# Unread products in six array tilings behind the last products of an attention and gated-layer kernel

## The chip, the cores and the metric

The kernel runs on one core of a Trainium2 chip. The metric is device time in microseconds (us). One execution was also recorded by the hardware profiler; its own time and its span (first to last recorded instruction) stand beside the runs below.

The engines are named as in the profile: PE is TensorE's products, PEld its weight loads, DVE VectorE, ACT ScalarE, POOL GpSimd, SP SyncE, which issues the transfers. A "q" behind a name means the engine's queue (semaphores, drains, issues).

## What is computed

One input `x` (2048 rows of 512) goes through two branches, which a gate mixes row by row:

```python
def reference(A_x, A_wq, A_wk, A_wv, A_wo, B_x, B_w_gate, B_w_up, B_w_down, gate_w):
    x = A_x
    g = sigmoid((x * gate_w).sum(-1, keepdims=True))
    # a: 32 query heads of 16, one key and one value head
    q = (x @ wq) in heads;  k = x @ wk;  v = x @ wv
    p = softmax(einsum("bhqd,bkd->bhqk", q, k) * 16 ** -0.5)
    a = (einsum("bhqk,bkd->bhqd", p, v) in rows) @ wo
    # b: gated layer of width 1792
    b = (sigmoid(x @ w_gate) * (x @ w_up)) @ w_down
    return g * a + (1 - g) * b
```

The kernel takes all of `x` from `A_x`, as the reference does.

## The kernel before

The rows of `x` are cut into four blocks of 512. Each block has eight units of attention (four heads of 512 queries each), 32 units in all. For a unit the kernel makes the scores twice: once to find each row's maximum (L1159 on TensorE, L1161 on VectorE), and once, turned, for the exponential (L1168, then L1170 on ScalarE). The products with the values and a column of ones (`v_aug`, L1029) give the outputs and their sums. Beside these run the products of the gated layer and of the output projection (`fill`, L1133).

Most operands are split into a high and a low part of type fp32r. Their products contract over 64 rows and stand in pairs, one in the upper half of the array's rows and one in the lower (`TOP` and `BOT`), each with a bank of its own in PSUM: a tiling of 64x128 (rows by columns of a tile). L1029's products are fp32, contract over 128 rows and have 32 columns: a tiling of 128x32, four tiles side by side. The trace writes such a product in fp32 as two records, one for each pass. The first projections (L874) take the whole array, 128x128.

The order of all this is a string of codes (`ORDER`, L683 to L729), which `plan` (L732) walks through; every engine then executes its part of that order in sequence. What follows the plan is written out by hand in `tile_kernel`, L1190 to L1227, for the last unit alone:

- L1192 names the bank of the last value products `end`, and the seven others `rest`; `ps` (L1193) are the last four of these.
- ScalarE copies `end` (L1196), TensorE turns it into `rest[0]` and `rest[1]` (L1198), VectorE divides by the sums (L1203, L1205), TensorE turns it back into `rest[2]` and `rest[1]` (L1207), and ScalarE copies that to `o_last` (L1209).
- The **last products** (L1214) project `o_last`, 16 products of the tiling 64x32 over 512 columns, into the four banks `ps`.
- VectorE (L1224), and for one tile ScalarE and GpSimd (L1220, L1221), add the four banks to the four output tiles `ba`, and SyncE stores them by five transfers (L1227).

Behind that comes a closing that the framework makes (in the profile under L1274): SyncE waits for the transfers that are under way, each engine drains, and all meet at a barrier before the program ends.

In the change two operands appear that the kernel has held since its first phase: `ks` (128 rows of 2048, fp32r), the keys, in both halves of the rows, and `v_aug` (128 rows, 16 groups of 32 columns, fp32). `turns` and `pairs` are views that reorder 512 columns as two interleaved runs of 256.

Of the kernel before, what the change touches and what calls it, by code (L numbers as in the profile page):

```python
# [18 lines left out]
P = 128  # L19
# [15 lines left out]
TOP, BOT = slice(0, 64), slice(64, 128)  # L35
HALF = (TOP, BOT)
# [705 lines left out]
def tile_kernel(ctx, tc, x_in, wq, wkv, wo, wg, wu, wd, consts_in, out):  # L742
    nc = tc.nc
# [18 lines left out]
    turns = lambda a: a.rearrange("p (w c) -> p c w", w=2)  # L762
    pairs = lambda a: a.rearrange("p (c w) -> p c w", w=2)
# [125 lines left out]
    v_aug = cp.tile([P, NC, 32], F32, name="v_aug")  # L889
# [16 lines left out]
    for o in (0, 64):  # L906
        nc.vector.tensor_copy(stack_of[:, :, o:o + 48].rearrange("p kc (i d) -> p kc i d", d=DH),
                              some[:, :, :DH].unsqueeze(2).to_broadcast([P, KC, 3, DH]))
        n = 8 if o else 9
# [4 lines left out]
    ks = cp.tile([P, S], F32R, name="ks")  # L914
# [277 lines left out]
    end, rest = banks[end], [bank for i, bank in enumerate(banks) if i != end]  # L1192
# [17 lines left out]
    for i in range(2):  # L1210
        for j in range(4):
            for t in (2 * i, 2 * i + 1):
                r, m = HALF[t % 2], slice(32 * j, 32 * j + 32)
                nc.tensor.matmul(pairs(ps[t][m, :]), o[i][r, m], turns(WS["last"][r]), start=True, stop=True)  # L1214
    BL = [BA.pop((NB - 1, t)) for t in range(NT)]
    for t in (1, 0, 2, 3):
        ba, g = BL[t], gsig[:, n0 + t:n0 + t + 1]
        if t == 1:
# [6 lines left out]
    for t in (0, 2, 1, 3):  # L1225
        for r in (slice(0, D // 2), slice(D // 2, D)) if t == 0 else (slice(0, D),):
            nc.sync.dma_start(out[(n0 + t) * P:(n0 + t + 1) * P, r], BL[t][:, r])  # L1227

# [49 lines left out]
```

## Time and profile before

| | us |
|---|---|
| median of 3 runs (lowest to highest) | 1533.65 (1532.41 to 1535.66) |
| the profiled execution's own time | 1534.46 |
| its span | 1532.7 |
| busy: TensorE products / weight loads | 1520.6 / 977.4 |
| busy: VectorE / ScalarE / GpSimd | 1359.3 / 1160.1 / 624.5 |

In a row of the timeline stand: start in us from the span's start, length of the merged group in us, engine, line, operation, output and inputs, the tiling (rows*columns of a tile), the shape, the number of records, and in brackets the engine's idle time ahead of it and what ended it. Ends of products are modelled, so that products which follow each other overlap in the records. In the instructions of a line stand: engine, operation, number, shortest/median/longest duration in ns, and the first and last start. In the stretches stand: the stretch and its length, busy time of the five rows PE, PEld, DVE, ACT, POOL with their counts, TensorE's granted clock, the share of the transfer engines and GB/s.

### The profile page before, as it was taken

The numbers are of one execution on the slowest core, as the hardware profiler recorded it, in microseconds if no ns is written. First come the engines' busy times: TensorE is split into PE (matmuls) and PEld (weight loads), VectorE is DVE, ScalarE is ACT, GpSimd is POOL, SyncE is SP. The second block draws the span as 40 slices with busy tenths as digits, with TensorE's granted clock in tenths as the row PEclk, the third lists the DMA queues.
The fourth block names the chain that finished last, engine by engine and source line by source line (L and its number), as shares of the span: only waits on it lengthen the run. The fifth ranks groups of instructions, "written<-read, shape, count | busy, mean of one in ns | idle before, by whom it ended". The sixth has DMA issues, their size and how long they took to land. (4 is left out here: it accounts for less than half of the span.)

```text
span 1532.7 us, 33127 instructions
## 1 busy us (share of the span) xinstructions
PE 1520.6 (99%) x12910; PEld 977.4 (64%) x12910; DVE 1359.3 (89%) x2320; ACT 1160.1 (76%) x2287; POOL 624.5 (41%) x585
## 2 busy tenths in 40 slices
PE   9999999999999999999999999999999999999997
PEld 7777666656655666666665666676665566666653
DVE  6999988999999998989899988989989998999742
ACT  4257777878788787778788787777878887868796
POOL 4361633561811163255263136077073115427141
PEclk9999999999999999999999999999999999999999
DMA  7531211221211121123031212013021112212011
GB/s 250 175 107 38 71 44 52 71 91 39 88 41 52 46 82 54 34 74 95 30 96 51 69 39 86 22 63 115 31 81 58 55 44 68 69 40 64 13 54 46
DMA packets 63218, 103.42 MB, mean 67 GB/s; under 512 B 24546, under 2 KB 25058, under 8 KB 63060
## 3 DMA queue, kind: packets, MB, share of 16 engines
q1 hardware_dynamic: 63060, 101.29, 20.8%
q8 instruction: 102, 1.67, 0.4%
q14 instruction: 56, 0.46, 0.1%
HBM read 79.51 MB, written 21.75 MB: 66 GB/s over the span
## 5 line engine op out<-in xcount | busy, mean ns | idle before, releaser
L1161 DVE TENSOR_REDUCE mx<-bank 128x1 f32<-128x512 f32 x2048 | 1249.3, 681 | 110.1 <-PE bank L1159 71.7
L1170 ACT ACTIVATE p<-bank 128x512 f32<-128x512 f32 x2048 | 1033.1, 653 | 84.4 <-PE bank L1168 43.9
L1168 PE MATMUL bank<-qs,ks 64*128 64x512 f32 x2048 | 683.1, 389 | 0.0
L1159 PE MATMUL bank<-ks,qs 64*128 64x512 f32 x2048 | 648.4, 394 | 0.8 <-DMA qs<-qd 0.8
L1029 PE MATMUL bank<-p,v_aug 128*32 128x512 f32 x4096 | 490.5, 598 | 0.0
L1168 PEld LDWEIGHTS bank<-qs,ks 64*128 64x128 f32 x2048 | 348.3, 185 | 108.6 <-DVE mx L1161 33.5
L1159 PEld LDWEIGHTS bank<-ks,qs 64*128 64x128 f32 x2048 | 332.2, 185 | 131.0 <-DVE mx L1161 52.1
L1029 PEld LDWEIGHTS bank<-p,v_aug 128*32 128x32 f32 x4096 | 108.3, 109 | 236.6 <-issue 203.0
L1133 PE MATMUL bank<-wd,hl 64*128 64x512 f32 x1344 | 250.5, 378 | 0.0
L1133 PE MATMUL bank<-x,wg 64*128 64x512 f32 x1344 | 247.8, 378 | 0.1
L1043 POOL TENSOR_TENSOR ou<-ou,ou 128x512 f32<-128x512 f32 x74 | 94.6, 1278 | 370.0 <-ACT ou L1036 370.0
L1133 PE MATMUL bank<-x,wu 64*128 64x512 f32 x1344 | 244.4, 378 | 0.1
L1036 ACT COPY ou<-bank 128x512 f32<-128x512 f32 x105 | 61.7, 588 | 226.2 <-PE bank L1029 187.2
L1133 PEld LDWEIGHTS bank<-wd,hl 64*128 64x128 f32 x1344 | 198.4, 186 | 16.7 <-issue 4.2
L1133 PEld LDWEIGHTS bank<-x,wg 64*128 64x128 f32 x1344 | 194.7, 186 | 16.3 <-issue 2.8
L1133 PEld LDWEIGHTS bank<-x,wu 64*128 64x128 f32 x1344 | 192.5, 186 | 15.6 <-POOL wg L851 1.7
L777 POOL TENSOR_TENSOR wd<-rd,wd 128x512 fp32r<-128x512 f32 x56 | 71.6, 1278 | 4.5
L777 POOL TENSOR_TENSOR hl<-h,hl 128x512 fp32r<-128x512 f32 x56 | 71.6, 1278 | 4.5
L1003 POOL CAST ms<-mm 128x16 fp32r<-128x16 f32 x32 | 6.3, 198 | 158.2 <-DVE mm L996 158.2
L851 POOL TENSOR_TENSOR wg<-rg,wg 128x1024 fp32r<-128x1024 f32 x28 | 66.4, 2370 | 5.7 <-ACT wg L841 3.6
L851 POOL TENSOR_TENSOR wu<-ru,wu 128x1024 fp32r<-128x1024 f32 x28 | 66.4, 2370 | 2.2
L776 POOL CAST hl<-h 128x512 fp32r<-128x512 f32 x56 | 34.2, 610 | 74.9 <-DVE h L1148 74.9
(78 smaller groups left out, 683.0 us busy)
## 6 DMA issues: line engine op xcount, KB each, us to landing
rg<-wg SPq DMA_DIRECT2D x28, 512.0 KB
ru<-wu SPq DMA_DIRECT2D x28, 512.0 KB
rd<-wd SPq DMA_DIRECT2D x28, 512.0 KB
qs<-qd SPq DMA_DIRECT2D x192, 64.0 KB
qd<-q SPq DMA_DIRECT2D x32, 256.0 KB
od<-ou SPq DMA_DIRECT2D x31, 256.0 KB
xf<-x_in SPq DMA_DIRECT2D x16, 256.0 KB
vd<-od SPq DMA_DIRECT2D x32, 128.0 KB
```

What stands on the lines that cost most here:

```text
L776: hi(hl[:, 0, :], raw)
L777: lo.tensor_tensor(hl[:, 1, :], raw, f32(hl[:, 0, :]), op=ALU.subtract)
L851: nc.gpsimd.tensor_tensor(WS[item][:, 1, :], raw, f32(WS[item][:, 0, :]), op=ALU.subtract)
L1003: nc.gpsimd.tensor_copy(hl[:, :, 0, :], mm)
L1029: nc.tensor.matmul(ps[32 * j:32 * j + 32, :], v_aug[:, c, :], PT.pop((u, c, j)), start=start, stop=stop)
L1036: nc.scalar.copy(to, ps)
L1043: nc.gpsimd.tensor_tensor(SUMS[u], SUMS[u], PARTS_OF[u].pop(0), op=ALU.add)
L1133: ins = nc.tensor.matmul(pairs(banks[i]), l, turns(r), start=start, stop=stop)
L1159: nc.tensor.matmul(pairs(banks[i]), qs_t[u % 3][r, pr, part(qt)], turns(ks[r, kb * 512:(kb + 1) * 512]), start=True, stop=True)
L1161: nc.vector.tensor_reduce(MX[u][:, pr, h, qt, kb:kb + 1], banks[i], axis=AX.X, op=ALU.max)
L1168: nc.tensor.matmul(pairs(banks[i]), ks[r, part(c)], turns(qs_t[u % 3][r, pr, :]), start=True, stop=True)
L1170: nc.scalar.activation(p, banks[i], AF.Exp, scale=0.25)
```

## The change

Behind the loop of the last products stands a new piece of code, and nothing else differs:

```diff
@@ -1212,6 +1212,24 @@
             for t in (2 * i, 2 * i + 1):
                 r, m = HALF[t % 2], slice(32 * j, 32 * j + 32)
                 nc.tensor.matmul(pairs(ps[t][m, :]), o[i][r, m], turns(WS["last"][r]), start=True, stop=True)
+    va = v_aug.rearrange("p c r -> p (c r)")
+    spots = [rest[0], rest[1]]
+
+    def rows64():
+        for h in (0, 1, 0, 1):
+            r = HALF[h]
+            nc.tensor.matmul(pairs(spots[h]), ks[r, 0:P], turns(ks[r, 512:1024]), start=True, stop=True)
+
+    def others(halves, cols, n):
+        spots_of = [(r, bank) for r, bank in zip((TOP, BOT) if halves else (slice(0, P),), spots)]
+        for m in range(0, P, cols):
+            for r, bank in spots_of:
+                nc.tensor.matmul(bank[m:m + cols, :n], va[r, m:m + cols], va[r, :n], start=True, stop=True)
+
+    rows64()
+    for halves, cols, n in ((True, 32, 256), (False, 32, 256), (True, 64, 256), (False, 64, 256), (True, P, P), (False, P, P)):
+        others(halves, cols, n)
+        rows64()
     BL = [BA.pop((NB - 1, t)) for t in range(NT)]
     for t in (1, 0, 2, 3):
         ba, g = BL[t], gsig[:, n0 + t:n0 + t + 1]
```

`rows64` is four fp32r products of the tiling 64x128 over 512 columns, two pairs. It stands seven times. Between stand six blocks of fp32 products from `v_aug`, one for each of the tilings 64x32 (8 products), 128x32 (4), 64x64 (4), 128x64 (2), all over 256 columns, and 64x128 (2) and 128x128 (1) over 128 columns: 49 products in all. They write the banks `rest[0]` and `rest[1]`, which nobody reads any more. The lines behind the new piece move down by 18 (L1224 becomes L1242, L1227 becomes L1245, L1274 becomes L1292).

On TensorE, at the end of its order, the difference begins so (`bank_72` and `bank_73` are `rest[0]` and `rest[1]`, `bank_78` and `bank_79` the last two of `ps`; the shapes are those of the output, partitions x columns):

```order
 L1214 MATMUL bank_78<-re_0_19490,o_last_19991 32x512
 L1214 MATMUL bank_79<-re_0_19490,o_last_19991 32x512
-L1274 UNCONDITIONAL_BRANCH
+L1221 MATMUL bank_72<-ks 128x512
+L1221 MATMUL bank_73<-ks 128x512
+L1221 MATMUL bank_72<-ks 128x512
+L1221 MATMUL bank_73<-ks 128x512
+L1227 MATMUL bank_72<-v_aug 32x256
+L1227 MATMUL bank_73<-v_aug 32x256
```

Where the program's branch to its closing stood right behind the last products, the first block of four and the first block of `v_aug` products stand now.

The same engine's last rows, from the fp32 block of the tiling 64x128 to the branch:

```order
+L1227 MATMUL bank_72<-v_aug 128x128
+L1227 MATMUL bank_73<-v_aug 128x128
+L1221 MATMUL bank_72<-ks 128x512
+L1221 MATMUL bank_73<-ks 128x512
+L1221 MATMUL bank_72<-ks 128x512
+L1221 MATMUL bank_73<-ks 128x512
+L1227 MATMUL bank_72<-v_aug 128x128
+L1221 MATMUL bank_72<-ks 128x512
+L1221 MATMUL bank_73<-ks 128x512
+L1221 MATMUL bank_72<-ks 128x512
+L1221 MATMUL bank_73<-ks 128x512
+L1292 UNCONDITIONAL_BRANCH
```

All of the added rows stand on TensorE, ahead of its branch. On SyncE the stores stand where they stood, under new line numbers:

```order
 L1073 DMA bc_19673<-rd_19793 64x1x512 x2
-L1227 DMA out<-ba_0_16465 128x256 x2
-L1227 DMA out<-ba_2_16622 128x512
-L1227 DMA out<-ba_1_16460 128x512
-L1227 DMA out<-ba_3_16627 128x512
-L1274 UNCONDITIONAL_BRANCH
+L1245 DMA out<-ba_0_16465 128x256 x2
+L1245 DMA out<-ba_2_16622 128x512
+L1245 DMA out<-ba_1_16460 128x512
+L1245 DMA out<-ba_3_16627 128x512
+L1292 UNCONDITIONAL_BRANCH
```

No transfer is added, removed or moved against another.

## The prediction

> **What bounds the kernel now.** I read the page's first lines, then the last microseconds in the timeline, then the queues' own end (semaphores and drains), because the change stands behind the last products and can only act there.
>
> ```profile
> span 1532.7 us, 33127 instructions
> PE 1520.6 (99%) x12910; PEld 977.4 (64%) x12910; DVE 1359.3 (89%) x2320; ACT 1160.1 (76%) x2287; POOL 624.5 (41%) x585
> ```
>
> TensorE is busy in 1520.6 of 1532.7 us, so for nearly the whole span more work for it would be paid in full. The end is another matter:
>
> ```profile
> 1523.80 2.39 PE L1214 MATMUL bank<-re,o_last 64*32 64x512 f32 x32
> 1524.36 0.15 PEld L1214 LDWEIGHTS bank<-re,o_last 64*32 64x32 f32 x8 [0.38 <-ACT o_last L1209]
> 1524.90 0.15 PEld L1214 LDWEIGHTS bank<-re,o_last 64*32 64x32 f32 x8 [0.39 <-issue]
> 1525.19 0.88 DVE L1224 SCALAR_TENSOR_TENSOR ba<-bank,gsig,ba 128x256 f32<-128x256 f32 x2 [1.72 <-PE bank L1214]
> 1525.30 0.69 ACT L1220 ACTIVATE pa_last<-bank,gsig 128x512 f32<-128x512 f32 x1 [1.07 <-PE bank L1214]
> 1525.71 3.65 SPq L1227 DMA_DIRECT2D out<-ba  x5
> 1526.06 1.26 POOL L1221 TENSOR_TENSOR ba<-ba,pa_last 128x512 f32<-128x512 f32 x1 [15.06 <-ACT pa_last L1220]
> 1526.28 1.41 DVE L1224 SCALAR_TENSOR_TENSOR ba<-bank,gsig,ba 128x512 f32<-128x512 f32 x2 [0.20 <-PE bank L1214]
> ```
>
> The last products (L1214) end at 1523.80 + 2.39 = 1526.19. Behind them come the additions on VectorE (to 1526.28 + 1.41 = 1527.69) and five stores issued by SyncE (to 1525.71 + 3.65 = 1529.36). TensorE has nothing in the last 6.5 us. What ends the span shows in the instructions of the closing line L1274, and in the DMA queue's waits:
>
> ```profile
> L1274 SPq EVENT_SEMAPHORE  x7: 17/28/2202, 1529.4 to 1532.6; - x7
> L1274 POOLq EVENT_SEMAPHORE  x4: 17/17/17, 1532.0 to 1532.6; - x4
> L1274 SPq DRAIN  x3: 7/7/7, 1531.9 to 1532.2; - x3
> L1274 PEldq DRAIN  x2: 13/994/1975, 1524.4 to 1532.3; - x2
> ```
> ```profile
> SPq L1274 <- DMA out<-ba: 2.2, 1, 2.2
> ```
>
> SyncE waits 2.2 us for the stores to land, drains at 1531.9, and GpSimd gathers all engines at 1532.0. From there to 1532.7 is a fixed closing of 0.7 us that every engine joins. TensorE's first drain begins at 1524.4; of its two durations it must be the 1.975 us one (the other begins at 1532.3, 0.4 us before the end), so TensorE reports done at 1524.4 + 1.975 = 1526.3. **It is early by 1531.9 - 1526.3 = 5.6 us.** That is the cover: added TensorE time is free up to 5.6 us, and every microsecond beyond it moves the end by one.
>
> **The change, part by part.** It removes and moves nothing. It adds 28 products of form 64x128 over 512 columns in seven blocks of four, and between them six blocks of `v_aug` products. They write banks whose readers were done before the last products could start, so no new wait stands on TensorE; the additions, stores and waits of the other engines stay as they were. The output banks of the last products are not touched.
>
> *The 64x128 blocks.* The trace has this very pattern: four half-height products between two runs of L1029, and again in the first phase between full-height products.
>
> ```profile
> 1516.01 1.07 PE L1029 MATMUL bank<-p,v_aug 128*32 128x512 f32 x8
> 1517.01 0.70 PE L1168 MATMUL bank<-qs,ks 64*128 64x512 f32 x4
> 1517.64 0.64 PE L1029 MATMUL bank<-p,v_aug 128*32 128x512 f32 x4
> ```
> ```profile
> 27.64 0.70 PE L1159 MATMUL bank<-ks,qs 64*128 64x512 f32 x4
> 28.27 2.86 PE L874 MATMUL bank<-x,wq 128*128 128x512 f32 x12
> 31.05 0.91 PE L1159 MATMUL bank<-ks,qs 64*128 64x512 f32 x5
> ```
>
> Start to start a block of four takes 1517.64 - 1517.01 = 0.63 us, and 28.27 - 27.64 = 0.63. What a change of tiling takes of that is seen against a stretch without one:
>
> ```profile
> 1513.22 0.38 PE L1168 MATMUL bank<-qs,ks 64*128 64x512 f32 x1
> ...
> 1513.43 0.38 PE L1168 MATMUL bank<-qs,ks 64*128 64x512 f32 x1
> 1513.44 0.59 PE L1133 MATMUL bank<-we,o 64*128 64x512 f32 x2
> 1513.65 0.38 PE L1168 MATMUL bank<-qs,ks 64*128 64x512 f32 x1
> 1513.87 0.38 PE L1133 MATMUL bank<-we,o 64*128 64x512 f32 x1
> 1513.87 0.38 PE L1168 MATMUL bank<-qs,ks 64*128 64x512 f32 x1
> 1514.17 1.07 PE L1029 MATMUL bank<-p,v_aug 128*32 128x512 f32 x8
> ```
>
> Pairs (one product in each half of the rows) follow at about 0.215 us (1513.22, .43, .65, .87); the pair ahead of another tiling holds the next start off by 0.30 (1513.87 to 1514.17), so a switch costs about 0.09. Two pairs are 0.43; the remaining 0.2 of a block is the switch behind it and the first weights, loaded in the open (0.11).
>
> *The blocks between.* A run of eight L1029 records is two passes over 512 columns (four column tiles side by side) and takes 1517.01 - 1516.01 = 1.00. Its passes come at:
>
> ```profile
> 1518.10 0.13 PEld L1029 LDWEIGHTS bank<-p,v_aug 128*32 128x32 f32 x4 [0.30 <-issue]
> 1518.53 0.13 PEld L1029 LDWEIGHTS bank<-p,v_aug 128*32 128x32 f32 x4 [0.30 <-issue]
> 1518.95 0.13 PEld L1029 LDWEIGHTS bank<-p,v_aug 128*32 128x32 f32 x4 [0.30 <-ACT p L1170]
> ```
>
> That is 0.43 a pass, and 1.00 - 0.86 = 0.14 for coming and going. Over 256 columns I halve the pass, 0.215:
> - 128x32, four products: 0.43 + 0.14 = **0.57**. The form is in the trace; only its length is not.
> - 64x32, eight products: L1214 has this form, and its passes come at 0.54 (1524.36 to 1524.90). If the rate is lower, a pass over 256 columns takes 0.27 and the block 0.68; if 0.11 is a fixed price of a pass, 0.43 + 0.22 + 0.14 = 0.79. I take **0.72**.
> - 64x64 (four products) and 128x64 (two): neither is in the trace. Below, the 128x32 block's 0.57; above, the dear 64x32 reading, 0.79. 128x64 fills the full height like 128x32 and has only longer weights (some 0.03 more in the open): **0.60**. 64x64 has both halves of the rows: **0.65**.
> - 64x128 over 128 columns in fp32: the tiling of its neighbours, so I count no switch. Two passes at half of 0.215 are 0.22, with a little for weights **0.25**, and the neighbours save one switch and one bare weight load, 0.2. If a change of type were a switch too, it would be 0.42 with nothing saved.
> - 128x128 over 128 columns in fp32: the nearest rows are four transposes of that size,
>
> ```profile
> 39.37 0.66 PE L946 MATMUL bank<-consts,vt 128*128 128x128 f32 x4
> 39.83 2.83 PE L874 MATMUL bank<-x,wkv_s 128*128 128x512 f32 x12
> ```
>
>   0.46 for four, some 0.11 each. Two passes, a switch and bare weights: 0.22 + 0.09 + 0.09 = **0.40**, between 0.33 and 0.50.
>
> *The sum.* In the rows above the next tiling starts 0.07 before the modelled end of the run ahead (1516.01 + 1.07 = 1517.08 against 1517.01), so the first added product starts at 1526.19 - 0.07 = 1526.12. Six blocks of four: 6 x 0.63 = 3.78. The blocks between: 0.72 + 0.57 + 0.65 + 0.60 + 0.25 + 0.40 - 0.2 = 2.99. The last block of four ends 0.70 after its start. TensorE's last product ends at 1526.12 + 3.78 + 2.99 + 0.70 = 1533.59. Its drain follows 0.1 behind (1526.3 against 1526.19), and I allow 0.1 for one more semaphore on SyncE (they take 17 to 28 ns with the steps between): 1533.8 in place of 1531.9. **The end moves by about +1.9 us**, from a span of 1532.7 to 1534.6. With the cheap ends (0.57, 0.57, 0.57, 0.57, 0.22, 0.33, less 0.2) it is 1.5; with the dear ones (0.79, 0.60, 0.79, 0.79, 0.42, 0.50, nothing saved) 2.8.
>
> The profiled execution took 1534.46, 1.8 more than its span; by it the change gives 1536.4. It lies 0.8 above the median of the three runs, 1533.65, so on the scale of the runs I say 1533.65 + 1.9 = **1535.6**, 0.12% more. One may ask whether TensorE still runs at its full clock so late:
>
> ```profile
> 1530.00:1530.50 0.50, 0.00 (x0) 0.00 (x0) 0.00 (x0) 0.00 (x0) 0.00 (x0) 1.00 1.04 393
> 1530.50:1531.00 0.50, 0.00 (x0) 0.00 (x0) 0.00 (x0) 0.00 (x0) 0.00 (x0) 0.66 0.16 57
> ```
>
> The granted clock (third figure from the end) holds 1.00 to 1530.5, over 4 us after the last product, and falls only then. With TensorE kept at work it should not fall.
>
> *A rule against the trace.* The rows above price a switch at 0.09 us. The Trainium skill, "TensorEngine Tiling (Array Packing)", Key Properties, says that a change of tiling mode, not merely of tile, drains the array. The trace agrees that it costs, and shows that the drain mostly hides behind the tail of the products ahead; by a rule of free switches, 12 x 0.09 = 1.1 us would fall out of the sum and leave +0.8.
>
> **The rivals.**
> 1. *All of it is hidden.* If neither switches nor first weights cost anything, the blocks are bare streaming: seven at 0.43, four at 0.43, two at 0.22 are 5.2 us; with 0.16 for the last product to run out (0.38 - 0.215) TensorE ends near 1531.5 and the stores still land last: +0, 1533.65. For it: SyncE's wait for the stores is the longest at the end. Against it: 0.63, not 0.43, for a block of four, in two places. That the products are not there at all would look the same, but they stand in TensorE's order.
> 2. *The unseen tilings are dear; it ends slower.* The switches into and out of 64x64 and 128x64, out of 64x32 and around the fp32 64x128 block are in no row. If at these eight the array ran empty (0.38 - 0.215 = 0.16 of tail) and weights were then loaded bare (0.19, the length of L874's loads below), each would take 0.35 in place of 0.1: 8 x 0.25 = +2.0, in all +3.9, or 1537.6. It decides from 1.2 us above my sum, where the bound of 0.2% (3.07 us, about what a measurement of this kernel can tell from no change) is passed. Against it: the two kinds of switch that the trace has, between 64x128 and 128x32 and between 64x128 and 128x128, cost the same.
>
> ```profile
> L874 PEld LDWEIGHTS bank<-x,wq 128*128 128x128 f32 x192 | 35.5, 189 | 8.0 <-DVE mx L1161 2.1 <-issue 1.3
> ```
>
> L874's products have one row group, each weight load takes 189 ns, and yet twelve take 31.05 - 28.27 = 2.78, or 0.23 each: the loads lie under the products. The Trainium skill, "TensorE: Matmul & The Clock Gate", Part 3 ("The mechanism"), says that a weight load overlaps products in flight only when its row group differs. By that, the weights of the second pass would stand bare in each of the six blocks between, some 6 x 0.19 = 1.1 us, and the sum would be +3.0; here the trace disagrees, so the rule lends the second rival only a little.
>
> **How the numbers follow.** Forecast 0.75, hidden 0.08, dear tilings 0.17. The forecast's own ends (1.5 and 2.8) stay within 0.2%, though 2.8 with the scatter of a median (the three runs span 3.3 us) may be read beyond it; so slower by over 0.2% gets 0.17 and a little more, 0.20, faster only scatter, 0.02, and within 0.2% 0.78. The range reaches from the hidden case to the dear one, 1533.6 to 1537.7.
>
> **What would show it.** In the changed profile: the first added product at about 1526.1, blocks of four at 0.63 start to start, the blocks between at 0.4 to 0.8, TensorE's last product near 1533.6, SyncE's wait at the closing ended by TensorE and not by a store, the stores and additions where they were, and 0.7 us of closing. It would be wrong if an unseen tiling took a microsecond, if the clock fell below 1.00 within the blocks, or if the stores landed later than before.

## The result, and the profile after

| | before | changed |
|---|---|---|
| median of 14 runs each (us) | 1533.40 (1532.30 to 1536.27) | 1536.16 (1535.34 to 1538.37) |
| ratio of the runs | | 1.0017, 95% interval 1.0010 to 1.0024 |
| span of the profiled execution | 1532.7 | 1534.4 |

The ratio is +2.6 us (1.5 to 3.7). The forecast was +1.9, and 1536.16 lies in its range of 1533.6 to 1537.7. Its likeliest case, within 0.2%, fits the middle of the interval (0.17%); the upper end, 0.24%, lies beyond it.

The chain of work that ended last names the added blocks one by one (start, us, engine, output, line, records). In the changed kernel:

```profile
1526.36 0.63 PE bank L1221 x4
1526.99 0.59 PE bank L1227 x16
1527.58 0.63 PE bank L1221 x4
1528.21 0.57 PE bank L1227 x8
1528.78 0.63 PE bank L1221 x4
1529.41 0.59 PE bank L1227 x8
1530.00 0.63 PE bank L1221 x4
1530.63 0.58 PE bank L1227 x4
1531.21 0.63 PE bank L1221 x4
1531.84 0.22 PE bank L1227 x4
1532.07 0.43 PE bank L1221 x4
1532.50 0.42 PE bank L1227 x2
1532.92 0.63 PE bank L1221 x4
```

A block of four 64x128 products costs 0.63 each time but one: behind the fp32 block of the same tiling it costs 0.43. There neither a switch nor bare weights are paid. The chain cuts its pieces at modelled ends; the starts in the trace say the same without them: the pair ahead of that fp32 block is followed after 0.216 us, like a pair ahead of another pair, while pairs ahead of another tiling are followed after 0.31. So a change of type within a tiling is no switch. The six blocks between cost 0.59 (64x32), 0.57 (128x32), 0.59 (64x64), 0.58 (128x64), 0.22 (64x128) and 0.42 (128x128). TensorE ends at 1532.92 + 0.63 = 1533.55.

SyncE's waits at the closing (engine and line, for whom, us in total, times, longest), in the changed kernel:

```profile
SPq L1292 <- PE bank L1221: 2.5, 1, 2.5
SPq L1292 <- DMA out<-ba: 1.9, 1, 1.9
```

The wait for the stores is still there, and the last wait is now for TensorE. Its closing line in that trace:

```profile
L1292 SPq EVENT_SEMAPHORE  x8: 17/28/2477, 1528.9 to 1534.3; - x8
L1292 POOLq EVENT_SEMAPHORE  x4: 17/17/17, 1533.7 to 1534.3; - x4
...
L1292 SPq DRAIN  x3: 7/7/7, 1533.6 to 1533.9; - x3
...
L1292 PEldq DRAIN  x2: 13/1219/2425, 1531.2 to 1534.0; - x2
```

TensorE's drain ends at 1531.2 + 2.4 = 1533.6, SyncE's begins at once, and the closing takes the 0.7 us it took before. The granted clock stays at 1.00 through the added blocks:

```profile
1533.00:1533.50 0.50, 0.50 (x4) 0.14 (x4) 0.00 (x0) 0.00 (x0) 0.00 (x0) 1.00 0.00 0
```

So the mechanism is the forecast one. What needed explaining was the size: every block came out as priced or a little cheaper (the 128x128 one 0.02 dearer), and yet the kernel lost 2.6 us and not 1.9.

### The profile page after: what moved, and what is told of

It is laid out like the page before. It is cut to its first block, busy times and chain, and to the rows that moved or that the text cites. A ratio compares the mean times of both kernels' runs of the same rounds, so it can differ in the third digit from the quotient of the medians.

```text
span 1534.4 us, 33268 instructions
## 1 busy us (share of the span) xinstructions
PE 1528.0 (100%) x12980; PEld 980.5 (64%) x12980; DVE 1359.4 (89%) x2320; ACT 1160.2 (76%) x2287; POOL 624.5 (41%) x585
```

## The experiments

In the following diffs the base is the changed kernel, unless they are copies. Theory A is the prediction's; B to D are its rivals after the result.

**Half of the blocks** (`e1_half`), which must fit under the cover:

```diff
-    for halves, cols, n in ((True, 32, 256), (False, 32, 256), (True, 64, 256), (False, 64, 256), (True, P, P), (False, P, P)):
+    for halves, cols, n in ((True, 32, 256), (False, 32, 256)):
```

> Leaves out the last four of the six fp32 blocks and the 64x128 blocks behind them: 24 added products in place of 49. Theory A (TensorE's added work is free until the stores have landed, and is paid in full beyond that): by the durations of the changed kernel's trace the last added product ends 3.1 us behind the last products (0.63 + 0.59 + 0.63 + 0.57 + 0.70), while the stores land 4.6 to 5.5 us behind them, so +0 (ratio 1.000, within 0.0005), SyncE's last long wait ends by a store. Theory B (the added products cost wherever they stand, through instruction fetch or by slowing the additions and stores, in proportion to their number): half of +2.7, so +1.3 us.

Measured against the kernel before: 1.0001 (0.9992 to 1.0010), so +0.2 us (-1.2 to 1.5). SyncE's waits in its trace have no row for products, only

```profile
SPq L1292 <- DMA out<-ba: 2.0, 1, 2.0
```

Twenty-four products under the cover cost nothing that can be measured. The interval alone does not exclude B's +1.3. The trace speaks against it: TensorE's last product ends at 1530.33 + 0.70 = 1531.03, the wait for the stores at 1532.26, and the span 5.29 us behind the last products, where the unchanged kernel's ends 5.2 to 5.3 behind them in three of four profiles (table below).

**One tiling** (`e2_one_tiling`), the same streaming without switches:

```diff
-    rows64()
-    for halves, cols, n in ((True, 32, 256), (False, 32, 256), (True, 64, 256), (False, 64, 256), (True, P, P), (False, P, P)):
-        others(halves, cols, n)
+    for _ in range(12):
         rows64()
```

> Replaces the six fp32 blocks by 64x128 blocks of the same streaming time: 48 products, 24 pairs, one tiling throughout. Theory A with the price of a switch and of first weights in the open: pairs follow at 0.215, 0.32 + 22 x 0.215 + 0.38 = 5.4 us from the first start to the last end against 7.26 in the changed kernel, so TensorE ends 1.8 us earlier than there, about when the stores land: +0.2 to +0.9 us against the kernel before. If switches and first weights are free: as the changed kernel, +2.7. Theory B (by number of products): +2.7.

Measured: 1.0005 (0.9996 to 1.0014), +0.8 us (-0.6 to 2.1). Its chain has one piece for all 48 products:

```profile
1528.65 5.38 PE bank L1221 x48
```

5.38 us, against 1533.55 - 1526.36 = 7.19 in the changed kernel: five excursions into another tiling and back, with the first weights, are 1.8 us, 0.36 each. Without them most of the loss goes, though TensorE still ends last, by

```profile
SPq L1290 <- PE bank L1221: 0.6, 1, 0.6
```

The span ends 6.24 us behind the last products, against 8.04 in the changed kernel: the same 1.8. B, which counts products, needed +2.7 for as many.

**The blocks twice** (`e3_twice`):

```diff
-    for halves, cols, n in ((True, 32, 256), (False, 32, 256), (True, 64, 256), (False, 64, 256), (True, P, P), (False, P, P)):
+    for halves, cols, n in 2 * ((True, 32, 256), (False, 32, 256), (True, 64, 256), (False, 64, 256), (True, P, P), (False, P, P)):
```

> The six fp32 blocks and the 64x128 blocks behind them stand twice. Theory A: beyond the cover every microsecond counts in full; one turn of the six takes 6.56 us in the changed kernel's trace (1526.29 to 1532.85), so 6.56 more than the changed kernel, +9.2 us against the kernel before. Theory B (by number of products, 94 for 49): +5.2.

Measured: 1.0060 (1.0047 to 1.0072), +9.2 us (7.2 to 11.0). SyncE's waits:

```profile
SPq L1292 <- PE bank L1221: 9.4, 1, 9.4
```

The wait for TensorE grows from 2.5 to 9.4, by the 6.56 us of a second turn and the 0.3 by which the wait began earlier. Beyond the cover everything counts in full.

**The same blocks ahead of the last products** (`e4_ahead`; here the base is the kernel before, and the piece is cut in its middle):

```diff
+    va = v_aug.rearrange("p c r -> p (c r)")
...
+        rows64()
     for i in range(2):
         for j in range(4):
             for t in (2 * i, 2 * i + 1):
```

> The same 49 products stand ahead of the last products instead of behind them. Theory A: there nothing covers them; the first pair waits for the copy of the second half of o_last (until about 0.5 us behind the present start of the last products), then 7.2 us of blocks, so the last products and all that follows start 7.2 to 7.8 us later: +7.2 to +7.8 us, with the tail behind the last products unchanged at 6 to 6.5 us. Theory B: +2.7, as the changed kernel.

Measured: 1.0054 (1.0039 to 1.0070), +8.3 us (6.0 to 10.7). The timeline of its trace gives the shift without that scatter:

```profile
1522.04 0.71 PE L1198 MATMUL bank<-consts,ou_last 128*128 128x128 f32 x4 [0.48 <-ACT ou_last L1196]
...
1531.52 2.39 PE L1232 MATMUL bank<-re,o_last 64*32 64x512 f32 x32
```

From the turned copies to the last products it takes 9.48 us, against 1523.80 - 1521.97 = 1.83 in the first profile of the kernel before (its L1198 starts at 1521.97): +7.65, as A expected. One part of the expectation failed: the tail behind the last products was not 6 to 6.5 us. They end at 1531.52 + 2.39 = 1533.91 and the span at 1539.1, so it was 5.2. The half-kernel's tail was as short, 5.3. This pointed at the profile of the kernel before itself.

**Three more profiles of the kernel before** (`b1`, `b2`, `b3`), unchanged copies, for the two theories on the missing microsecond:

> The kernel before again, for a second profile of its end. Theory C (the cover itself varies: the profiled execution of the kernel before took 1534.46, 1.1 more than the typical 1533.4, because its last store was issued over 1.40 us and landed late): here the stores land 4.5 to 5.5 us behind the last products, and where no store that stands late in the queue is issued slowly, about 4.6, with a span of about 1531.7. Theory D (the scatter comes from the stretch ahead of the last products): the tail behind the last products is 6.5 us as before, whatever the span.

> The kernel before a third time. Theories C and D as for the second profile: C expects the tail behind the last products to differ between executions by up to 1 us with the store that is issued slowly, D expects 6.5 us each time.

> The kernel before a fourth time. Theories C and D as for the second profile: C expects the tail behind the last products to differ between executions by up to 1 us with the store that is issued slowly, D expects 6.5 us each time.

The issues of the five stores in the second profile (shortest/median/longest, in ns), SyncE's wait for them, and the drains of SyncE and TensorE:

```profile
L1227 SPq DMA_DIRECT2D out<-ba x5: 332/376/423, 1526.3 to 1528.5; - x5
```
```profile
SPq L1274 <- DMA out<-ba: 1.9, 1, 1.9
```
```profile
L1274 SPq DRAIN  x3: 7/7/7, 1531.2 to 1531.5; - x3
L1274 PEldq DRAIN  x2: 13/998/1983, 1524.9 to 1531.6; - x2
```

And in the first profile, on which the prediction stood:

```profile
L1227 SPq DMA_DIRECT2D out<-ba x5: 332/376/1402, 1525.7 to 1528.0; - x5
```

In both profiles the fifth issue begins 1.77 us behind the last products. In the first it takes 1.00 us longer (1.40 against 0.40), and the long wait behind it 0.28 longer (2.20 against 1.93): together the 1.28 by which the tails differ. So C is right about the tail. It is not right about whole times: it expected a span of about 1531.7, and the three are 1532.0, 1532.4 and 1532.1, because the last products begin later; and `b1` took 1534.84, more than the first profiled execution's 1534.46, with no slow issue.

**Two more profiles of the changed kernel** (`a1`, `a2`):

> The changed kernel again, for a second profile of its end. If its end hangs on TensorE alone, the tail behind the last products is 8.0 us whether or not a store is issued slowly (first profile: 8.04, with one store issued over 1.12 us). If it still hangs on the stores, the tail varies by up to 1 us, as that of the kernel before does (5.2, 5.2, 5.3 and 6.5 us).

> The changed kernel a third time, with the same two readings as for its second profile: 8.0 us again if TensorE alone sets the end, up to 1 us of variation if the stores still do.

The executions whose end bears on this, in one table. "Tail" runs from the end of the last products to the end of the span.

| profile | last products begin | longest store issue (us) | tail (us) | last long wait of SyncE |
|---|---|---|---|---|
| before, first | 1523.80 | 1.40 (the fifth) | 6.50 | stores |
| `b1` | 1524.39 | 0.42 | 5.22 | stores |
| `b2` | 1524.85 | 0.42 | 5.21 | stores |
| `b3` | 1524.36 | 0.42 | 5.33 | stores |
| `e1_half` | 1525.59 | 0.46 (the second) | 5.29 | stores |
| `e4_ahead` | 1531.52 | 0.42 | 5.22 | stores |
| `e2_one_tiling` | 1526.26 | 1.16 (the second) | 6.24 | TensorE |
| `e3_twice` | 1524.19 | 0.56 (the second) | 14.60 | TensorE |
| changed, first | 1523.97 | 1.12 (the second) | 8.04 | TensorE |
| `a1` | 1524.01 | 0.70 (the second) | 8.04 | TensorE |
| `a2` | 1525.95 | 0.70 (the second) | 8.04 | TensorE |

In the first profile of the changed kernel the last products stand at

```profile
1523.97 2.39 PE L1214 MATMUL bank<-re,o_last 64*32 64x512 f32 x32
```

and the span ends at 1534.4. The kernel before ends 5.2 to 5.3 us behind its last products in three profiles, and 6.5 only in the one that the prediction was read from. The changed kernel ends 8.04 behind them in three of three, whatever its stores do; twice the blocks add 14.60 - 8.04 = 6.56, as their length says. The difference is 8.04 - 5.25 = 2.8 us, and the runs gave 2.6 (1.5 to 3.7). Theory D is not empty either: with the same work ahead of them, the last products begin from 1523.8 to 1524.9 in the four profiles of the kernel before, and from 1524.0 to 1526.3 in those with products added behind them; the spans scatter with that. The change stands behind that stretch, and the tails alone account for the measured difference; that the stretch adds nothing to it is not shown by itself.

**Views of the last products** (`e5_views`), for a term of the sum that came out too high. Between 64x128 blocks stand four blocks of the tiling 64x32 over 512 columns:

```diff
+    same = lambda a: a
     rows64()
-    for halves, cols, n in ((True, 32, 256), (False, 32, 256), (True, 64, 256), (False, 64, 256), (True, P, P), (False, P, P)):
-        others(halves, cols, n)
+    for out_view, in_view in ((same, same), (same, turns), (pairs, same), (pairs, turns)):
+        for m in range(0, P, 32):
+            for r, bank in zip(HALF, spots):
+                nc.tensor.matmul(out_view(bank[m:m + 32, :]), va[r, m:m + 32], in_view(va[r, :]), start=True, stop=True)
         rows64()
```

> Behind the last products stand four blocks of the tiling 64x32 over 512 columns, between 64x128 blocks: plain, with the moving operand in the interleaved view, with the output in the paired view, and with both as the last products have them. The question is why the last products' passes came at 0.54 us while the changed kernel's 64x32 block ran at about 0.24 for 256 columns. If a view makes the pass slower: blocks with that view take 0.2 us more than the plain one (about 1.2 against 1.0). If the rate of 64x32 over 512 columns is lower whatever the views: all four about 1.2. If it was the last products' own waits or weights: all four about 1.0.

The timeline of its TensorE, in the order plain, interleaved input, paired output, both:

```profile
1528.31 1.09 PE L1234 MATMUL bank<-v_aug 64*32 64x512 f32 x16
1529.33 0.70 PE L1221 MATMUL bank<-ks 64*128 64x512 f32 x4
1529.96 1.31 PE L1234 MATMUL bank<-v_aug 64*32 64x512 f32 x16
1531.19 0.70 PE L1221 MATMUL bank<-ks 64*128 64x512 f32 x4
1531.82 1.09 PE L1234 MATMUL bank<-v_aug 64*32 64x512 f32 x16
1532.84 0.70 PE L1221 MATMUL bank<-ks 64*128 64x512 f32 x4
1533.47 1.31 PE L1234 MATMUL bank<-v_aug 64*32 64x512 f32 x16
1534.71 0.70 PE L1221 MATMUL bank<-ks 64*128 64x512 f32 x4
```

Start to the next start the blocks take 1.02, 1.23, 1.02 and 1.24. The interleaved moving operand costs 0.21 in two passes, 0.11 a pass; the paired output costs nothing; the tiling as such is as fast as 128x32 (1.00).

## Why the prediction was right, and where its size was off

- **The path.** "It is early by 1531.9 - 1526.3 = 5.6 us" and "every microsecond beyond it moves the end by one": right as a mechanism. Half of the blocks cost nothing that can be measured, twice the blocks cost another 6.6 us, and ahead of the last products they cost all of their 7.65.
- **The cover was the mis-sized term.** 5.6 us was read from one execution, and it was that execution's own. Its fifth store was issued over 1.40 us, and the wait for it ended late. In `b1` TensorE's drain ends at 1524.9 + 1.98 = 1526.9, 0.1 behind the last products as before, and SyncE drains at 1531.2: 4.3 us. The row with 1402 ns as its longest issue was there to be read beside the median of 376. That the profiled time lay 0.8 above the median was no sign of it: `b1` took longer still with the short tail. I carried the profiled difference over to the median as if both ends scattered alike; but behind the last products the changed kernel's end hangs on TensorE, whose work there takes the same 7.19 us each time, while the old end hangs on the stores, which scatter.
- **The blocks.** Forecast 0.63 for a block of four: 0.63 in six of seven places, and 0.43 at the place where I saved 0.2. Blocks between: 0.72, 0.57, 0.65, 0.60, 0.25, 0.40 forecast, 0.59, 0.57, 0.59, 0.58, 0.22, 0.42 measured. The one clear miss, 64x32, came from the last products' rate of 0.54 a pass; `e5_views` shows that their interleaved operand makes that rate, which the added block does not have. TensorE's end came 7.19 behind the last products, against 1533.59 - 1526.19 = 7.40 forecast.
- **The sum of the errors.** The tail was forecast at 1534.6 - 1526.2 = 8.4 and is 8.04, 0.4 too long; the tail of before was taken as 6.5 and is mostly 5.25, 1.25 too long. The two leave the forecast 0.9 short, +1.9 for +2.8. They pull in opposite directions, so it was partly luck that the forecast came this close: with the blocks priced as they ran and the cover as read, it would have been +1.5.
- **The rivals.** "All of it is hidden" fell on the switches: `e2_one_tiling`, in which there are none, is 1.8 us shorter on TensorE. "The unseen tilings are dear" fell as well: into and out of 64x64 and 128x64 a block costs what it costs at 128x32, 0.57 to 0.59. The price of a switch, 0.09, held too (0.31 against 0.215 behind a pair), but the 12 switches counted for a sum without them are one too many: the fp32 block of the tiling 64x128 is no change, which leaves 11, about 1.0 us. And the weights of a second pass lay under the products, as the prediction read from L874: the single 128x128 fp32 product, with two passes in the same rows, took 0.42, and a second load of 189 ns in the open would have made it about 0.6.
- **The closing.** SyncE does wait for TensorE by one more semaphore (eight for seven in its closing row), as allowed for, but that wait comes last and SyncE drains within 0.1 of TensorE's end.

## What to carry to other kernels

The room behind an engine's last instruction is a difference of two ends, and each has a scatter of its own; it should be read from several executions, or at least checked for one that is longer than its median within a row (1402 against 376 ns here). Work that is added under such a cover cost nothing up to the cover and its full length beyond, in these runs. The tail behind a fixed event measured that more finely than the whole time: for the changed kernel it repeated to 0.01 us where the runs spread over 3. An excursion of TensorE from the tiling 64x128 into another and back cost about 0.36 us here (0.34 to 0.40 for the five tilings tried), first weights included.

## What the runs showed of the hardware

- Beyond its streaming (two passes of 0.215, or 0.11 for 128 columns) a block cost 0.14 to 0.16 at 64x32, 128x32, 64x64 and 128x64, and 0.20 at 128x128, where the starts in the trace show 0.11 of first weights in the open and 0.10 of switch. The forms that the trace of before lacked are no dearer than the others. A change from fp32r to fp32 within 64x128 cost nothing.
- An fp32 moving operand read in two interleaved runs took 0.11 us more for a pass over 512 columns in the tiling 64x32. The fp32r products of the main loop read theirs in the same view, and their pairs follow at 0.215.
- A slow store issue went with a transfer of instructions. In the first profile of the kernel before, the transfers from 1526 to 1530 us have among their queues

```profile
q8 instruction: 1, 0.02, 1.5%
```

  and in `b1` there is no such row from 1526 to 1530. Eight profiles have such a transfer during the issues. In each, the issue that was under way when the transfer ended lasted 0.36 to 0.40 us beyond that end, about the length of an issue alone. In seven of them it was the second issue, which began 0.1 before the end of the last products, and it was longer the later the transfer ended:

| profile | transfer ends, us behind the last products | that issue (us) | it ends |
|---|---|---|---|
| `e1_half` | 0.01 | 0.46 | 0.37 |
| `e3_twice` | 0.11 | 0.56 | 0.47 |
| `a1` | 0.24 | 0.70 | 0.61 |
| `a2` | 0.24 | 0.70 | 0.61 |
| changed, first | 0.65 | 1.12 | 1.04 |
| `e5_views` | 0.66 | 1.14 | 1.06 |
| `e2_one_tiling` | 0.70 | 1.16 | 1.07 |
| before, first | 2.80 | 1.40 | 3.17 |

  Every issue with no such transfer under way took 0.33 to 0.42 us. Being under way together is not enough, though: in those seven the first issue ran under the same transfer, at least for its end, and took 0.34. In the first profile of the changed kernel the slow second issue put the last one off by 0.3 us, and the wait for the stores ended as much later, still ahead of TensorE; in the first profile of before the slow one was the last. This was seen and not tried: no run moved the transfer on purpose, so that it causes the slow issue is only argued.
